# A forward transform by remainders of d mod 4, with a quarter of the frequencies in its tables, in a fused spectral and feed-forward kernel

## The chip, the cores and the metric

The kernel runs on one core of a Trainium2 chip. The metric is the device time of one execution in microseconds (us), here the median of three runs of the same program. A profile is one execution taken by the hardware profiler; its span is a little shorter than the measured time (1389.4 against 1391.22 us) and its inner times are used for the working. Engines are named as the profile names them: PE for the matrix engine's matmuls, PEld for its weight loads, DVE for the vector engine, ACT for the scalar engine, POOL for GpSimd, SP for the engine that issues most of the DMA transfers.

## The reference

Forward and backward of a gated mix of two branches over an input of 2048 rows (S) by 576 columns (D), bf16. Branch a multiplies the 2-D Fourier transform of `x` by learned weights and transforms back. Branch b is a feed-forward block with a gated GELU over 4608 inner columns.

```python
def _A_ref(x, w_r, w_i):
    X = jnp.fft.rfft2(x.astype(jnp.float32), axes=(-2, -1))
    X = X * (w_r + 1j * w_i)
    return jnp.fft.irfft2(X, s=(S, D), axes=(-2, -1)).astype(jnp.bfloat16)

def _B_ref(x, w_gate, w_up, w_down):
    return (_gelu(x @ w_gate) * (x @ w_up)) @ w_down

g = _sigmoid((x * gate_w).sum(-1, keepdims=True))
out = g * _A_ref(A_x, A_w_r, A_w_i) + (1 - g) * _B_ref(B_x, ...)   # with x = A_x for the gate
# ... and the gradients of out for A_x, A_w_r, A_w_i, the three B weights and gate_w
```

The change lies in the forward half of the spectral branch. There, `x` and the incoming gradient are both transformed: first over D (576 real points, of which the frequencies 0 to 288 are kept, so DF = 289), then over S.

## The kernel before

The kernel is one long stream of matmuls. The feed-forward block goes in 18 groups (`g`) of 256 inner columns, each in four pairs (`m`) of 512 rows. A pair computes `z` (the gradient times the down weight), `xy` (the input times the gate and up weights), and then the weight gradients of the group before it (`wps` matmuls, called jobs). Between those jobs, units of the spectral branch are dropped in one at a time by `fft_next()`; each takes a tile of the PSUM pool that `z` uses too, and that pool has one buffer.

The forward transform has two kinds of unit for each of 16 row groups `t` and each of two sources, so 32 of each. `u1` transforms over D by products with tables of cosines and sines. Even and odd `d` are kept apart (`par`), with half of the frequencies (HF = 145) in each table; the other half follows from sums and differences. `u2` transforms over a part of S and then forms those sums and differences on DVE.

```python
HF = 145
def eo(c):                      # columns of chunk c: even d for c = 0, 2, odd d for c = 1, 3
    return slice(256 * (c % 2) + c // 2, 256 * (c % 2) + 256, 2)
...
def u1(t):
    def f():
        yps = ps()
        for par, j in [(par, j) for par in range(2) for j in range(2)] + [(0, 2), (1, 2)]:
            ci, tab = (4, 4 + 2 * (t % 2) + par) if j == 2 else (2 * par + j, 2 * par + j)
            nc.tensor.matmul(yps[:, par, :2 * HF], lhsT=src[:, ci, t, :], rhs=tb.Dt[tab].rearrange("p c l -> p (c l)"),
                             start=(j == 0), stop=(j == 2))
        ys[t] = unit([2, 2, HF], name="Y")
        ...                     # ACT copies yps to Y, in bf16, with a scale for the gradient
def u2(t):
    def f():
        ...
        for o, ys_ in enumerate((Yf[:, 0:4:3, :], Yf[:, 2:0:-1, :])):
            nc.tensor.matmul(vps[:, o, :2 * HF]..., lhsT=R, rhs=ys_, start=True, stop=True)
        ve = unit([2, 2, HF], F32, name="ve")
        nc.scalar.copy(ve..., vps[:, :, :2 * HF])
        V.tensor_tensor(Vt[:, :, 0:HF], v[0], v[1], op=ALU.add)
        V.tensor_tensor(Vt[:, :, DF - 1:HF - 1:-1], v[0][:, :, 0:HF - 1], v[1][:, :, 0:HF - 1], op=ALU.subtract)
        LD.dma_start(dst[:, t], Vt[:])
```

The chunks of `d` are 128 + 128 + 128 + 128 + 64 columns; the last one, 512 to 575, has tables of its own (tabs 4 to 7), zero for the half of the partitions that belongs to the other row group of its pair. The order of `d` on the partitions is also that of the feed-forward weights: `load_w` brings `w_gate` and `w_up` in this order, and turns `w_down` by a transposing transfer into `wtmp`, from which four transfers within SBUF pick every second partition:

```python
def load_w(g, part, tails=LD):  # called with part 0, 1, 2 at the ends of pairs m = 0, 1, 2
    ...
    elif part == 1:
        wtmp[0] = wpool.tile([P, 4, FG], BF16, tag="wtmp", name="wtmp", bufs=1)
        ...
        LD.dma_start_transpose(wtmp[0][:], B_w_down[fsl, 0:512])
    else:
        ...
        for par in range(2):
            for h, r in enumerate((LO, HI)):
                LD.dma_start(wdT[r, 2 * par:2 * par + 2, :], wtmp[0][par:P:2, h:4:2, :])
```

Three places decide the order of emission that the change touches. `turned(h)` transposes eight tables `Rt`, and in its first call the two tables `B` as well, into the same PSUM tile; ACT copies the eight, DVE the two. `run_late(tb)` makes those `Rt` tables with sines on ACT, and from there on in that pair the results of the jobs are copied out by DVE. The pacing loop spreads the `n` spectral units of a pair evenly over its jobs:

```python
tables = {6: 1}.get(pr)         # pair 6: run_late ahead of job 1
for i, (w, f) in enumerate(jobs):
    if k < n and (at >= max(total * k / n - 0.45, free) or len(jobs) - i <= n - k):
        free = at + (1.7 if wide() else 0.0)
        fft_next()
        k += 1
    if i == tables:
        run_late(tb)
        wcopy[0] = VC
    f()
    at += w
```

The inverse transform has units `z` (`Z` and its copy `ZT`), `ztail` and `d`, sent by the same loop.

Of the kernel before, what the change touches and what calls it, by code (L numbers as in the profile page):

```python
# [10 lines left out]
ALU = mybir.AluOpType  # L11
# [29 lines left out]
HF = 145  # L41
NL = 2 * (HF - P)


def eo(c):

    return slice(256 * (c % 2) + c // 2, 256 * (c % 2) + 256, 2)
# [16 lines left out]
def iotas(nc, res, unit):  # L64
    tb = Tables()
    G, V = nc.gpsimd, nc.vector
    kw = dict(allow_small_or_imprecise_dtypes=True)
    tb.halfpi = res.tile([P, 1], F32, name="halfpi")
    V.memset(tb.halfpi[:], math.pi / 2)
    tb.pi = res.tile([P, 1], F32, name="pi")  # L70
    V.memset(tb.pi[:], math.pi * EPS_SCALE)
    tb.warm = res.tile([P, 1], F32, name="warm")
    nc.scalar.activation(tb.warm[:], tb.halfpi[:], ACT.Sin)
    tb.lrow = unit([HF], F32, name="lrow")
    G.iota(tb.lrow[:], pattern=[[1, HF]], base=0, channel_multiplier=0, **kw)
    tb.dcol = res.tile([P, 5], F32, name="dcol")
    for par in range(2):
        G.iota(tb.dcol[:, 2 * par:2 * par + 2], pattern=[[256, 2]], base=par, channel_multiplier=2, **kw)
    for r in (LO, HI):
        G.iota(tb.dcol[r, 4:5], pattern=[[0, 1]], base=512, channel_multiplier=1, **kw)  # L80
    tb.dn = res.tile([P, 5], F32, name="dn")
    V.tensor_scalar(tb.dn[:], tb.dcol[:], 1.0 / D, None, op0=ALU.mult)
    tb.late = []
    tb.Dt = []
    tb.Rt = []
    return tb


def iotas_R(nc, tb, res, unit):
    G, V = nc.gpsimd, nc.vector  # L90
    kw = dict(allow_small_or_imprecise_dtypes=True)
    tb.qcol_i = res.tile([P, 1], I32, name="qcol_i")
    G.iota(tb.qcol_i[:], pattern=[[0, 1]], base=0, channel_multiplier=1)
    kk = tb.kk = unit([2, P], F32, name="kk")
    tb.krow = kk[:, 0, :].rearrange("p (g k c) -> p g k c", k=2, c=2)
    for v in range(2):
        G.iota(tb.krow[:, :, v, :], pattern=[[1 - 2 * v, 32], [0, 2]], base=64 * v, channel_multiplier=0, **kw)
    G.memset(tb.krow[:, 0, 1, :], 32.0)
    tb.kadd = kk[:, 1, :].rearrange("p (k c) -> p k c", c=2)
    G.iota(tb.kadd, pattern=[[0, 64], [S // 4, 2]], base=S // 4, channel_multiplier=0, **kw)  # L100
    tb.scol = res.tile([P, T], F32, name="scol")
    G.iota(tb.scol[:], pattern=[[1, T]], base=0, channel_multiplier=16, **kw)
    par_i = res.tile([P, 1], I32, name="par_i")
    tb.par = res.tile([P, 2], F32, name="par_f")

    def parity():
        V.tensor_single_scalar(par_i[:], tb.qcol_i[:], 1, op=ALU.bitwise_and)
        V.tensor_copy(tb.par[:, 1:2], par_i[:])
        V.tensor_scalar(tb.par[:, 0:1], tb.par[:, 1:2], -1.0, 1.0, op0=ALU.mult, op1=ALU.add)
        V.tensor_scalar(tb.kadd[:, 0, 1:2], tb.par[:, 1:2], float(S // 2), float(S // 4), op0=ALU.mult, op1=ALU.add)  # L110
    return parity
# [7 lines left out]
def build_D(nc, tb, unit, c0, n):  # L119

    V = nc.vector
    step = 2.0 * math.pi / D
    TS = (nc.gpsimd if c0 else V).tensor_scalar
    X = unit([n, HF], F32, name="XD")
    y = unit([n, HF], F32, name="yD")
    for c in range(n):
        TS(y[:, c, :], tb.lrow[:], tb.dn[:, c0 + c:c0 + c + 1], MAGIC, op0=ALU.mult, op1=ALU.add)  # L130
    TS(y[:], y[:], -MAGIC, -float(D), op0=ALU.add, op1=ALU.mult)
    o = unit([n, 2, HF], name="Dt")

    def angles():
        for c in range(n):
            V.scalar_tensor_tensor(X[:, c, :], tb.lrow[:], tb.dcol[:, c0 + c:c0 + c + 1], y[:, c, :],
                                   op0=ALU.mult, op1=ALU.add)
        V.scalar_tensor_tensor(y[:], X[:], -1.0, X[:], op0=ALU.mult, op1=ALU.max)

    def sines():  # L140
        nc.scalar.activation(o[:, :, 0, :], y[:], ACT.Sin, bias=tb.halfpi[:], scale=-step)
        nc.scalar.activation(o[:, :, 1, :], X[:], ACT.Sin, scale=-step * EPS_SCALE)
        if c0 < 4:
            tb.Dt += [o[:, c] for c in range(n)]

    def tails():
        tl = unit([2, 2, 2, HF], name="Dt")
        nc.gpsimd.memset(tl[HI, 0], 0.0)
        nc.gpsimd.memset(tl[LO, 1], 0.0)
        for k, r in enumerate((LO, HI)):  # L150
            for par in range(2):
                V.tensor_scalar(tl[r, k, par], o[r, 0], tb.par[r, par:par + 1], None, op0=ALU.mult)
        tb.Dt += [tl[:, k, par] for k in range(2) for par in range(2)]
    return angles, sines, tails


# [99 lines left out]
def kernel(  # L256
# [23 lines left out]
    scr = [[dram.tile([4, P, FF], BF16, name=f"scr{k}_{m}") for m in range(T // 4)] for k in range(3)]  # L280
    a_scr = dram.tile([S, D], BF16, name="a_scr")
# [18 lines left out]
    def load_w(g, part, tails=LD):  # L300
# [4 lines left out]
        if part == 0:  # L305
            wgu = wts[g][0]
            for w, c0 in ((B_w_gate, 0), (B_w_up, FG)):
                cols = slice(c0, c0 + FG)
                LD.dma_start(wgu[:, 0:4, cols].rearrange("p (e k) f -> p e k f", e=2),
                             w[0:512, fsl].rearrange("(k p e) f -> p e k f", e=2, p=P))  # L310
                for r in (LO, HI):
                    tails.dma_start(wgu[r, 4, cols], w[512:D, fsl])
# [4 lines left out]
        else:  # L317
            wdT = wts[g][1]
            LD.dma_start(wdT[LO, 4, :], wdT[HI, 4, :])
            for par in range(2):  # L320
                for h, r in enumerate((LO, HI)):
                    LD.dma_start(wdT[r, 2 * par:2 * par + 2, :], wtmp[0][par:P:2, h:4:2, :])
# [282 lines left out]
    def fwd_units(src, dst, scale, ps=pftile):  # L605
        ys = {}

        def u1(t):
            def f():
                yps = ps()  # L610
                for par, j in [(par, j) for par in range(2) for j in range(2)] + [(0, 2), (1, 2)]:
                    ci, tab = (4, 4 + 2 * (t % 2) + par) if j == 2 else (2 * par + j, 2 * par + j)
                    nc.tensor.matmul(yps[:, par, :2 * HF], lhsT=src[:, ci, t, :], rhs=tb.Dt[tab].rearrange("p c l -> p (c l)"),  # L613
                                     start=(j == 0), stop=(j == 2))
                ys[t] = unit([2, 2, HF], name="Y")
                yo = ys[t][:].rearrange("p e c l -> p e (c l)")
                if scale is None:
                    nc.scalar.copy(yo, yps[:, :, :2 * HF])
                else:
                    nc.scalar.activation(yo, yps[:, :, :2 * HF], ACT.Copy, scale=scale[:, t:t + 1])  # L620
            return f

        def u2(t):
            def f():
# [3 lines left out]
                Yf = Y[:].rearrange("p e c l -> p (e c) l")  # L628
                for o, ys_ in enumerate((Yf[:, 0:4:3, :], Yf[:, 2:0:-1, :])):
                    nc.tensor.matmul(vps[:, o, :2 * HF].rearrange("p (e l) -> p e l", e=2), lhsT=R, rhs=ys_, start=True, stop=True)  # L630
                Vt = half([2, DF], name="Vt")
                ve = unit([2, 2, HF], F32, name="ve")
                nc.scalar.copy(ve[:].rearrange("p o c l -> p o (c l)"), vps[:, :, :2 * HF])
                v = [ve[:, 0], ve[:, 1]]
                V.tensor_tensor(Vt[:, :, 0:HF], v[0], v[1], op=ALU.add)
                V.tensor_tensor(Vt[:, :, DF - 1:HF - 1:-1], v[0][:, :, 0:HF - 1], v[1][:, :, 0:HF - 1], op=ALU.subtract)
# [4 lines left out]
    def tail_table():  # L641
# [4 lines left out]
        for k, r in ((2, P), (3, 32)):  # L646
            o = 512 * (k - 2)
            for c in range(2):
                nc.tensor.transpose(tp_[:, c, o:o + r], tb.Dt[k][0:r, c, 0:P], ident[0:r, 0:r])
            for c in range(2):  # L650
                nc.tensor.transpose(tp_[0:n, c, o + 256:o + 256 + r], tb.Dt[k][0:r, c, P:HF], ident[0:r, 0:r])
# [5 lines left out]
        for c in range(2):  # L657
            for e, sb in enumerate((tb.Dt[1], ot)):
# [5 lines left out]
    def turned(h):  # L664

        def f():
            tp_ = pftile(BF16)
            ts = range(8 * h, 8 * h + 8)
            for k, t in enumerate(ts):
                nc.tensor.transpose(tp_[:, 0, k * P:(k + 1) * P], tb.Rt[t], ident[:])  # L670
            o = unit([8, P], name="RT")
            nc.scalar.copy(o[:].rearrange("p t m -> p (t m)"), tp_[:, 0, :])
            if h == 0:
                for v in range(2):
                    nc.tensor.transpose(tp_[:, 1, v * P:(v + 1) * P], tb.B[:, v, :], ident[:])
# [160 lines left out]
    def inv_units(s, dv, scale):  # L836
# [14 lines left out]
        def z(p):  # L851
# [11 lines left out]
            f.wide = True  # L863
# [14 lines left out]
        def d(i):  # L878
            def f():
# [20 lines left out]
                LD.dma_start(dv[:, i, :], yo[:, 0:D])  # L900
            return f
# [18 lines left out]
    D0 = build_D(nc, tb, unit, 0, 2)  # L920
# [4 lines left out]
    D2 = build_D(nc, tb, unit, 2, 2)  # L925
    D2[0]()
    D4 = build_D(nc, tb, unit, 4, 1)
# [5 lines left out]
    titems(dB, dOT, 0, (None, None, phtile), (None, None, VC))[2]()  # L933
    D4[0]()
# [28 lines left out]

    def wide():
        return hasattr(next(u for u in fft[fft_pos[0]:] if not getattr(u, "noslot", False)), "wide")
# [48 lines left out]
    for g in range(NG):  # L1014
# [3 lines left out]
        for m in range(NPR):  # L1018
# [65 lines left out]
            else:  # L1084
# [32 lines left out]
                tables = {6: 1}.get(pr)  # L1117
                for i, (w, f) in enumerate(jobs):
                    if k < n and (at >= max(total * k / n - 0.45, free) or len(jobs) - i <= n - k):
# [20 lines left out]
            if m < 3 and g + 1 < NG:  # L1140
                load_w(g + 1, m)
# [247 lines left out]
```

## Time and profile before

| | |
|---|---|
| time, median of 3 (lowest to highest) | 1391.22 us (1391.06 to 1391.48) |
| span of the profiled execution | 1389.4 us, 26,012 instructions |
| granted PE clock | 1.0 of full speed all along |
| the 40 slices of the span | PE at nine tenths or more in every one |
| DMA, mean | 154 GB/s, 214.49 MB moved |
| where the forward transform lies | from 74 to 298 us (first `u1` matmul to last `Vt`) |

In the profile's rows `u1`'s matmuls are those of line L613 (`pf<-Dt`), `u2`'s those of L630, the jobs' L552, L570 and L584, `z`'s L424 and L429, `xy`'s L433 and L440, and the second half of the kernel, products with stored tiles, is L1239. Matmuls overlap one another in the array[...]. What one costs in a stream is the distance from its start to the start of the next, and the timeline gives that.

### The profile page before, as it was taken

To read this page: it belongs to the slowest core of one execution; us is meant where nothing else is said; L and a number is where in the kernel's file an instruction comes from. 1 tells how busy PE (TensorE), PEld (TensorE's weight loads), DVE (VectorE), ACT (ScalarE), POOL (GpSimd) and SP (SyncE) were. 2 spreads that over 40 slices of the span, in tenths; PEclk is the share of its full clock that TensorE was granted. 3 is DMA by queue.
4 is the path that set the end of the run, shared out by engine and by line. 5 is a ranking of instruction groups with operands and counts; after the bars stand their busy time and mean duration, and the time that the engine had idled before them with its cause. 6 is when DMAs were issued, how large, how long until landed. Compare 5 with 4: busy or idle time off the path is not lost.

```text
span 1389.4 us, 26012 instructions
## 1 busy us (share of the span) xinstructions
PE 1380.2 (99%) x10272; PEld 912.9 (66%) x10272; DVE 752.9 (54%) x1419; ACT 702.3 (51%) x1299; POOL 245.2 (18%) x486
## 2 busy tenths in 40 slices
PE   9999999999999999999999999999999999999999
PEld 7556556556556566556566566556777777777777
DVE  7976556555888877885767676560001742121111
ACT  7976767767878778866767666651000000000000
POOL 3001110123345634422110111110000110000000
PEclk9999999999999999999999999999999999999999
DMA  7424344355466556555556555759999998777773
GB/s 225 120 85 135 114 128 106 103 157 142 126 158 161 157 147 162 140 142 136 141 151 157 147 158 150 168 124 281 190 192 203 224 193 168 162 159 166 156 151 89
DMA packets 510791, 214.49 MB, mean 154 GB/s; under 512 B 312555, under 2 KB 503725, under 8 KB 510669
## 3 DMA queue, kind: packets, MB, share of 16 engines
q1 hardware_dynamic: 493546, 187.44, 58.0%
q0 software_dynamic: 14912, 24.24, 6.5%
q8 instruction: 80, 1.31, 0.4%
q10 hardware_dynamic: 2210, 1.15, 0.3%
q14 instruction: 43, 0.34, 0.1%
HBM read 41.05 MB, written 93.84 MB: 97 GB/s over the span
## 4 chain that ended last, share of the span: by engine, by line
PE 95%; DVE 3%; ACT 2%; issue 0%; POOL 0%; DVEq 0%; POOLq 0%; ACTq 0%
PE acc L1239 30%; PE xy L440 17%; PE wps L570 17%; PE wps L552 9%; PE z L424 9%; PE wps L584 2%; PE xy L433 2%; PE pf L613 2%; PE z L429 2%; PE pf L886 1%; PE pf L812 1%; PE pf L630 1%; PE pf L723 1%; PE pf L888 1%; PE pf L859 1%; PE pf L379 0%
## 5 line engine op out<-in xcount | busy, mean ns | idle before, releaser
L1239 PEld LDWEIGHTS <-pin 128*128 128x128 bf16 x3456 | 337.6, 98 | 86.2 <-issue 0.5
L570 PE MATMUL wps<-dH,xn 128*128 128x512 bf16 x1152 | 271.4, 379 | 1.1 <-DVE dwd L521 1.0
L440 PE MATMUL xy<-wgu,xT 128*128 128x512 bf16 x1152 | 270.6, 380 | 0.0
L440 PEld LDWEIGHTS <-xT 128*128 128x128 bf16 x1152 | 106.5, 98 | 132.8 <-issue 24.8
L570 PEld LDWEIGHTS <-xn 128*128 128x128 bf16 x1152 | 111.4, 98 | 119.7 <-issue 1.9
L1256 ACT COPY bo<-acc 128x288 f32<-128x288 f32 x32 | 12.7, 398 | 305.1 <-PE acc L1239 271.6
L552 PE MATMUL wps<-dB,A 128*128 128x288 bf16 x1152 | 153.8, 286 | 0.1
L577 POOL DMA_DIRECT2D out_dram<-dw x134 | 72.8, 547 | 431.1 <-ACT dw L521 390.0
L1239 PE MATMUL acc<-wgT,pin 128*128 128x288 bf16 x1152 | 143.8, 286 | 0.0
L1239 PE MATMUL acc<-wuT,pin 128*128 128x288 bf16 x1152 | 143.6, 286 | 0.0
L1239 PE MATMUL acc<-wd_all,pin 128*128 128x288 bf16 x1152 | 142.6, 286 | 0.0
L424 PE MATMUL z<-wdT,dOT 128*128 128x256 bf16 x1152 | 137.7, 273 | 0.6 <-ACT ZT L862 0.2
L552 PEld LDWEIGHTS <-A 128*128 128x128 bf16 x1152 | 112.1, 98 | 33.2 <-issue 0.3
L452 ACT ACTIVATE da<-z,omg 128x256 bf16<-128x256 f32 x288 | 112.0, 471 | 32.4 <-PE z L429 32.3
L424 PEld LDWEIGHTS <-dOT 128*128 128x128 bf16 x1152 | 112.3, 98 | 22.9 <-issue 1.7
L461 ACT CAST xb<-xy 128x512 bf16<-128x512 f32 x144 | 85.0, 590 | 49.8 <-PE xy L440 49.8
L1311 DVE SCALAR_TENSOR_TENSOR f32t<-gwf,dlog,b16t 128x576 f32<-128x576 f32 x16 | 13.1, 817 | 170.4 <-DMA b16t<-dxa_scr 170.4
L459 ACT ACTIVATE q<-xy 128x512 bf16<-128x512 f32 x144 | 87.8, 613 | 15.8 <-PE xy L440 14.5
L462 ACT CAST hu<-xy 128x512 bf16<-128x512 f32 x144 | 87.4, 607 | 0.0
L498 DVE TENSOR_TENSOR xb<-xb,sg 128x1024 bf16<-128x1024 bf16 x48 | 33.2, 691 | 94.3 <-ACT sg L490 94.2
L521 ACT CAST dw<-wps 128x512 bf16<-128x512 f32 x72 | 42.3, 589 | 55.4 <-PE wps L570 53.1
L1270 DVE SCALAR_TENSOR_TENSOR b16t<-b16t,g,f32t 128x576 bf16<-128x576 bf16 x16 | 13.1, 818 | 98.3 <-DMA b16t<-a_scr 98.1
(224 smaller groups left out, 1655.6 us busy)
## 6 DMA issues: line engine op xcount, KB each, us to landing
scr<-dH SPq DMA_DIRECT2D x144, 256.0 KB, 3.4
scr<-A SPq DMA_DIRECT2D x72, 256.0 KB, 2.5
out_dram<-dw POOLq DMA_DIRECT2D x134, 64.0 KB, 2.5
wd_all<-in_B_w_down_dram SPq DMA_DIRECT2D x3, 1728.0 KB, 9.4
out_dram<-dwd POOLq DMA_DIRECT2D x34, 144.0 KB, 3.1
scr_p<-Vt SPq DMA_DIRECT2D x32, 145.0 KB, 3.0
wgu<-in_B_w_gate_dram SPq DMA_DIRECT2D x18, 256.0 KB, 4.3
wgu<-in_B_w_up_dram SPq DMA_DIRECT2D x18, 256.0 KB, 3.3
```

The source lines that it names most:

```text
L424: nc.tensor.matmul(zo(t), lhsT=dOT[:, ci, t, :], rhs=wdT[:, ci, :], start=(t % 4 < 2 and ci == 0), stop=False)
L440: nc.tensor.matmul(xy[k][:, t % 2, :], lhsT=xT[:, ci, t, :], rhs=wgu[:, ci, :], start=False, stop=(ci == 3))
L452: nc.scalar.activation(da[:, t, :], z[:, t % 2, t // 2, :], ACT.Copy, scale=omg32[:, 4 * m + t:4 * m + t + 1])
L459: nc.scalar.activation(q[:, h, :], xy[:, :, 0:FG], ACT.Square)
L461: nc.scalar.copy(xb[:, h, :], xy[:, :, 0:FG])
L462: nc.scalar.copy(hu[:, h, :], xy[:, :, FG:2 * FG])
L498: V.tensor_tensor(xb[:], xb[:], s[:], op=ALU.mult)
L521: wcopy[0](out, in_)
L552: nc.tensor.matmul(wps[:, :288], lhsT=tl(0, t)[:, fch * P:(fch + 1) * P], rhs=dB[:, t, h * 288:(h + 1) * 288], start=(t == 0), stop=(t == ...
L570: nc.tensor.matmul(wps[:].rearrange("p a b -> p (a b)"), lhsT=xn[:, t, c * P:(c + 1) * P], rhs=kt[t // 4][1][:, t % 4].rearrange("p k f -> ...
L577: wst[0].dma_start(ov[:, c, fsl], dw[:, k, :])
L1239: nc.tensor.matmul(acc[:, :288], lhsT=src[:, r, :], rhs=w_of(r)[:, h * 288:(h + 1) * 288], start=(first and r == 0), stop=(last and r == F ...
```

## The change

The forward transform over D is rewritten so that the columns are sorted by `d mod 4` (`r` = 0, 1, 2, 3), and each table holds only a quarter of the frequencies (QF = 73). From the four remainders the frequencies l, 288 − l, 144 − l and 144 + l follow by sums and differences. Remainders 0 and 2 share one PSUM bank with their cosines and sines placed in crossed order, and so do 1 and 3, so that `u1` has four matmuls over a quarter (2 × 73 columns) and two over the tail chunk (4 × 73 columns, zeros where the remainder is another). `u2`'s two matmuls keep their form; its sums and differences take five DVE instructions where there were two, by way of a new fp32 tile `M`.

```diff
 HF = 145
+QF = 73
 def eo(c):
-    return slice(256 * (c % 2) + c // 2, 256 * (c % 2) + 256, 2)
+    return slice(c, 512, 4)
...
 def u1(t):
-                for par, j in [(par, j) for par in range(2) for j in range(2)] + [(0, 2), (1, 2)]:
-                    ci, tab = (4, 4 + 2 * (t % 2) + par) if j == 2 else (2 * par + j, 2 * par + j)
-                    nc.tensor.matmul(yps[:, par, :2 * HF], lhsT=src[:, ci, t, :], rhs=tb.Dt[tab].rearrange("p c l -> p (c l)"),
-                                     start=(j == 0), stop=(j == 2))
-                ys[t] = unit([2, 2, HF], name="Y")
+                for o in range(2):
+                    for r, bs in ((2 * o, slice(0, 4, 3)), (2 * o + 1, slice(1, 3))):
+                        nc.tensor.matmul(yps[:, o, 0:4 * QF].rearrange("p (b l) -> p b l", b=4)[:, bs, :], lhsT=src[:, r, t, :],
+                                         rhs=tb.D4[:, r], start=(r % 2 == 0), stop=False)
+                for o in range(2):
+                    nc.tensor.matmul(yps[:, o, 0:4 * QF], lhsT=src[:, 4, t, :],
+                                     rhs=tb.D4t[:, t % 2, o].rearrange("p b l -> p (b l)"), start=False, stop=True)
+                ys[t] = unit([2, 4 * QF], name="Y")
...
 def u2(t):
-                for o, ys_ in enumerate((Yf[:, 0:4:3, :], Yf[:, 2:0:-1, :])):
-                    nc.tensor.matmul(vps[:, o, :2 * HF].rearrange("p (e l) -> p e l", e=2), lhsT=R, rhs=ys_, start=True, stop=True)
+                for o in range(2):
+                    nc.tensor.matmul(vps[:, o, 0:4 * QF], lhsT=R, rhs=Y[:, o], start=True, stop=True)
...
-                V.tensor_tensor(Vt[:, :, 0:HF], v[0], v[1], op=ALU.add)
-                V.tensor_tensor(Vt[:, :, DF - 1:HF - 1:-1], v[0][:, :, 0:HF - 1], v[1][:, :, 0:HF - 1], op=ALU.subtract)
+                V.tensor_tensor(M[:, 0]..., ve[:, 0:4]..., ve[:, 4:8]..., op=ALU.add)
+                V.tensor_tensor(M[:, 1, 0], ve[:, 0:2], ve[:, 4:6], op=ALU.subtract)
+                V.tensor_tensor(M[:, 1, 1], ve[:, 6:2:-3], ve[:, 2:8:5], op=ALU.subtract)
+                up = Vt[:, :, 0:2 * (HF - 1)]...[:, :, :, 0:QF]
+                dn = Vt[:, :, DF - 1:0:-1]...[:, :, :, 0:QF - 1]
+                V.tensor_tensor(up, M[:, :, :, 0], M[:, :, :, 1], op=ALU.add)
+                V.tensor_tensor(dn, M[:, :, :, 0, 0:QF - 1], M[:, :, :, 1, 0:QF - 1], op=ALU.subtract)
```

The inverse transform still needs tables over even and odd `d`. So three such tables (columns 5 to 7 of `dcol`, 3 × 145) are built beside the four quarter ones (4 × 73), and their angles are now made wholly on POOL. The tail tables are 16 products of 64 × 73 on POOL, where there were four of 64 × 290 on DVE.

The order of `d` on the partitions changes for the feed-forward weights too. A partition now holds four neighbouring rows of the weight, and `w_down` gets there by way of a scratch in device memory, in one part more, and one pair later:

```diff
+    wscr = [dram.tile([512, FG], BF16, name=f"wscr{k}") for k in range(2)]
...
-                LD.dma_start(wgu[:, 0:4, cols].rearrange("p (e k) f -> p e k f", e=2),
-                             w[0:512, fsl].rearrange("(k p e) f -> p e k f", e=2, p=P))
+                LD.dma_start(wgu[:, 0:4, cols], w[0:512, fsl].rearrange("(p r) f -> p r f", r=4))
...
-            for par in range(2):
-                for h, r in enumerate((LO, HI)):
-                    LD.dma_start(wdT[r, 2 * par:2 * par + 2, :], wtmp[0][par:P:2, h:4:2, :])
+            LD.dma_start(wscr[g % 2][:].rearrange("(c p) f -> p c f", p=P), wtmp[0][:])
+        else:
+            LD.dma_start(wts[g][1][:, 0:4, :], wscr[g % 2][:].rearrange("(p r) f -> p r f", r=4))
...
-                load_w(g + 1, m)
+                for part in ((0, 1), (2,), (3,))[m]:
+                    load_w(g + 1, part)
```

Three changes concern the order of emission alone: the transposes of `B` move to the second call of `turned`; the sines of pair 6 come ahead of job 2, not job 1; and in the pacing loop the last unit of a pair may be sent earlier, so that some job time (2.0 for the units `z` and `d` of the inverse transform) is left behind it.

```diff
-            if h == 0:
+            if h == 1:
                 for v in range(2):
                     nc.tensor.transpose(tp_[:, 1, v * P:(v + 1) * P], tb.B[:, v, :], ident[:])
...
-                tables = {6: 1}.get(pr)
+                last = getattr(upcoming(n - k0)[-1], "last", 0.0) if n > k0 else 0.0
+                tables = {6: 2}.get(pr)
                 for i, (w, f) in enumerate(jobs):
-                    if k < n and (at >= max(total * k / n - 0.45, free) or len(jobs) - i <= n - k):
+                    if k < n and (at >= max(min(total * k / n - 0.45, total - last - 0.9 * (n - 1 - k)), free) or len(jobs) - i <= n - k):
```

The number of PE instructions stays the same (10,272 matmuls, each with its weight load).

## The prediction

> **What bounds the kernel now.** I read the busy line of the page first, then the waits of PE, then the timeline of PE.
>
> ```profile
> PE 1380.2 (99%) x10272; PEld 912.9 (66%) x10272; DVE 752.9 (54%) x1419; ACT 702.3 (51%) x1299; POOL 245.2 (18%) x486
> ```
>
> PE is busy for 99% of the span; DVE and ACT for about half. A busy PE need not be one at its peak, so the next question is whether it waits. The waits of PE (engine, line, waited for: total us, times, longest):
>
> ```profile
> PE pf L914 <- POOL ident masks.py:199: 1.4, 1, 1.4
> PE pf L675 <- ACT RT L672: 1.1, 1, 1.1
> PE wps L570 <- DVE dwd L521: 1.0, 1, 1.0
> PE pf L723 <- ACT Xg L728: 0.5, 1, 0.5
> PE pf L613 <- ACT ve L633: 0.4, 2, 0.2
> PE z L424 <- ACT ZT L862: 0.2, 1, 0.2
> PE pf L379 <- DVE dOT L386: 0.2, 1, 0.2
> ```
>
> Together 4.8 us of 1389. So the time is the length of the matmul stream, and only two things shorten it: fewer columns through the array, or these few waits gone. The timeline of PE shows what a unit takes in the stream (start, duration of the merged piece, count at the end; I use the distances between starts):
>
> ```profile
> 87.29 0.91 PE L613 MATMUL pf<-Dt,xT 128*128 128x290 bf16 x6
> 88.04 1.02 PE L440 MATMUL xy<-wgu,xT 128*128 128x512 bf16 x4
> 88.90 1.03 PE L570 MATMUL wps<-dH,xn 128*128 128x512 bf16 x4
> ...
> 654.97 0.23 PE L886 MATMUL pf<-Dt,ZT 128*128 128x145 bf16 x1
> 655.03 0.23 PE L886 MATMUL pf<-Oi,ZT 128*128 128x145 bf16 x1
> 655.10 0.29 PE L888 MATMUL pf<-At,ZU 68*128 68x290 bf16 x1
> 655.23 0.23 PE L886 MATMUL pf<-Dt,ZT 128*128 128x145 bf16 x1
> ```
>
> A `u1` of six matmuls takes 88.04 − 87.29 = 0.75 us, 125 ns for each 290 columns. Four of 512 take 0.86 us, 215 ns each. The inverse transform already has matmuls of half the width, each with new weights: two of 145 columns take 655.10 − 654.97 = 0.13 us, 65 ns each, and one of 290 takes 0.13. So narrow matmuls with a fresh weight load still cost by their columns.
>
> **What the Trainium skill says.** "TensorE: Matmul & The Clock Gate", section "Back-to-back issue gap", gives a warm gap of N/2.4 + 2.5 ns for N columns: 63 ns for 145 and 123 for 290, and the trace agrees (65 and 125). The same section says that a real stream with weight loads is slower, about 81 ns for 128 columns; here eight of 128 columns (L859) take from 651.93 to 652.38 on the timeline, 56 ns each, so I go by the trace. "PSUM — Partial Sum Buffer", "The four PSUM rules", says that the first matmul of a group clears the written-marks of its whole bank, and later ones overwrite where no mark is set. That is why one start flag for each bank is enough in the new `u1`, although its second remainder writes other columns: no extra matmul is needed. No view of a trace shows these marks. "VectorE: DVE Perf Modes", on the trn2 errata, gives (N + 151)/0.96 ns for an fp32 addition of two tensors; for `u2`'s 290 and 288 elements that is 459 and 457 ns, and the trace has 460 and 452 (lines below). "ScalarE: Activation LUTs", "What ACT_TABLE_LOAD costs", has about 1283 ns for a load; the trace has 1.28 us for each, at 77.25 and at 81.52.
>
> **The change part by part.**
>
> 1. `u1`, on the path. Before: 6 × 290 = 1740 columns, 0.75 us. After: 4 × 146 + 2 × 292 = 1168 columns. By the trace's neighbours: 4 × 65 ns + 2 × 126 ns = 0.51 us. Saved 0.24 us in each of 32 units: **7.7 us**. `u2`'s 292 columns for 290, in 64 matmuls, at (215 − 125)/222 = 0.4 ns a column, give back 0.05 us.
>
> 2. `u2`'s sums on DVE, beside the path. The groups of DVE between 74 and 300 us:
>
> ```profile
> L635 DVE TENSOR_TENSOR Vt<-ve 128x290 bf16<-128x290 f32 x32 | 14.7, 460 | 39.4 <-ACT ve L633 36.8 <-DMA wtmp<-in_B_w_down_dram 2.2
> L636 DVE TENSOR_TENSOR Vt<-ve 128x288 bf16<-128x288 f32 x32 | 14.4, 452 | 0.0
> ```
>
> Each `u2` has 0.91 us of DVE now, and DVE comes to it idle (36.8 us of waiting for `ve`). After: sums over 292, 146, 146, 292 and 288 elements. With the section's formula that is an estimate of 461 + 309 + 309 + 461 + 457 = 2.0 us, so 1.09 more in each, 35 us in all. The windows from 74 to 313 us have DVE busy for 145.9 of 239 us, 61%; with 35 more 76%. Only the transfer of `Vt` waits for these sums, and `Vt`'s readers come much later. I count nothing for it on the path.
>
> 3. ACT copies 584 columns where it copied 580. Nothing.
>
> 4. The sines of pair 6. On the timeline the 32 matmuls of L552 start at 75.24 and the next line follows at 80.37, after the wait on the DVE copy `dwd`. 32 of them need 3.9 us elsewhere (8 in 0.98), so 1.2 us are lost. ACT is in its sines from 77.25 to 81.52, and DVE, which takes both copies meanwhile, is in a run of table and GELU work until 79.86. With the sines one job later, ACT copies the first result ahead of them and its buffer is free for L570: **1.2 us**.
>
> 5. `turned`. The eight transposes of L670 start at 300.79 and need 0.45 us, but L675 starts at 302.50, after ACT's copy of `RT` (301.44 to 302.45), which reads the same tile: 1.26 us lost. After the change four jobs of 0.86 us lie between, from 301.24 to 302.10; the second `turned` then needs the one PSUM buffer, still read until 302.45, so some 0.4 us stay. Saved **0.85 us**.
>
> 6. The last unit of a pair. Comparing the orders of the matmuls, beside `u1` and `turned` only five pairs of the inverse transform change, by one job's shift of a unit. They hold three visible losses, where `z` comes soon after a unit on its buffer: 780.53 to 781.79 for four of 512 (0.86 needed), and 793.87 to 795.13 and 807.66 to 808.93 for eight of 288 (0.98 needed). That is 0.40 + 0.28 + 0.29, together **1.0 us**.
>
> 7. The opening, 0 to 35 us. DVE loses 1.0 us of tail products and two of its angle steps; it gains one absolute value over 3 × 145. POOL gains three rows of angles, by its rows (145 wide 0.42 us each, 290 wide 0.44) some 4.5 us in all, done near 7 us, while DVE wants them after 8.1. ACT's sines of 290 become 435, so the gate's sigmoid comes some 0.4 us later. I take the balance as zero, with half a microsecond either way. The 16 tail products on POOL are wanted only at 74 us.
>
> 8. The weights by way of `wscr`: two transfers for four, issued one pair (12 us) ahead of `z`, where a landing takes 2.7 us. Hidden.
>
> Sum: −7.7 + 0.05 − 1.2 − 0.85 − 1.0 = −10.7 us. Moved units tend to make some new small wait, and the opening may lose a little; I leave 0.6 us for that. 1391.2 − 10.1 = **1381.1 us**.
>
> **The rivals.** (a) *DVE becomes the limit*: its sums delay the GELU products that stand behind them in its queue, and through them the jobs. For it: 76% is much, and the queue is in order. Against it: the products of a pair feed jobs of the next group, four pairs later, and PE waits for DVE only once in the trace outside the opening. It would give back 2 to 6 us, so about 1384 to 1387. (b) *The saved columns turn into waits*: `u1` and `u2` share one PSUM buffer, and ACT's copies of 0.64 to 0.74 us set when it is free; four jobs of 0.86 us between units just cover that. In the trace a unit waits there seldom (0.4 us for L613). A shorter `u1` doesn't shorten the cover, since the jobs between stay. Were each of 32 units to lose 0.1 us, 3 us would go: 1384. (c) *The narrow matmuls are bound by weight loads* of 98 ns each: then 4 × 98 + 2 × 126 = 0.64 us, and only 3.4 us are saved: 1385. The 65 ns of L886, with loads of its own, speaks against it. (d) *Opening or weights come late*: a stall of POOL's angles holds DVE's `xT` copies and PE for 1 to 2 us. (e) *Everything moves well*: all waits of parts 4 to 6 vanish and the opening gains: 1379.5.
>
> **Range and chances.** The middle is 1381.1. (e) sets the lower side, with some extra room; (a) to (d), each of perhaps one chance in ten, the upper: 1378 to 1386. Two per cent are 27.8 us, nearly three times the whole sum, so neither verdict of 2% is likely: 0.01 for faster, 0.98 for within, 0.01 for slower.
>
> **What would show it.** `u1`'s group in the timeline at 0.50 to 0.52 us from start to the next (c wrong); PE's busy time lower by about 8; the waits on `dwd` and of L675 gone, a wait of the second `turned` of about 0.4 in their place; DVE at some 76% between 74 and 300 with no PE wait on it (a wrong); ACT idle ahead of `ve` as before (b wrong). The prediction is wrong if PE shows new waits on DVE or on `ve`, if the narrow matmuls take 80 ns or more, or if the first 35 us grow by over 1 us.

## The result, and the profile after

The changed kernel takes 1384.03 us (1383.99 to 1385.74) against 1391.14 us on the same chips: a ratio of 0.9952, 95% interval 0.9939 to 0.9965. That is 7.1 us less; the prediction's middle was 10.1 less. The range holds it, but 3 us of the expected gain are missing, and the question is where.

The busy line of the page after, and the longest waits of PE in it:

```profile
PE 1363.2 (99%) x10186; PEld 908.5 (66%) x10272; DVE 783.2 (57%) x1514; ACT 701.6 (51%) x1300; POOL 259.8 (19%) x513
```

```profile
PE xy L460 <- issue: 6.8, 43, 0.2
PE pf L943 <- POOL ident masks.py:199: 1.4, 1, 1.4
PE pf L651 <- ACT Y L640: 1.1, 1, 1.1
PE pf L633 <- ACT ve L655: 1.0, 2, 0.7
PE pf L399 <- DVE dOT L406: 0.8, 1, 0.8
...
PE pf L697 <- ACT RT L702: 0.2, 1, 0.2
```

Two things must be read with care. This profile has 10,186 matmul records where the program has 10,272; 69 of the missing ones are `xy` matmuls of L460. A missing record looks like an idle engine, and the first line, 43 times 0.16 us ahead of L460, is of that kind: the distance from start to start at those places is that of the matmuls before and one unseen. Two later profiles (that of the iotas sent first, and that of pair 7's own `q` with the sines put back, both below) have all 10,272 records, and there this line is gone. For the same reason PE's busy time in this profile can't be compared with that of before. What can be compared are the starts of the same matmuls. I take the first `z` matmul of each of the 72 pairs (L424 before, L444 after) from the two timelines:

| start of pair (us) | before | after | difference | what lies in between |
|---|---|---|---|---|
| 0 | 7.86 | 7.73 | −0.13 | first loads |
| 3 | 36.98 | 37.74 | +0.76 | the opening |
| 6 | 66.56 | 67.38 | +0.82 | |
| 7 | 82.09 | 81.47 | −0.62 | pair 6: sines moved, one `u1` |
| 8 | 94.10 | 94.77 | +0.68 | pair 7: two `u1` |
| 22 | 289.32 | 283.45 | −5.86 | 0.46 less in nearly every pair, each with two `u1` |
| 23 | 305.65 | 298.92 | −6.73 | `turned` |
| 59 | 767.95 | 761.31 | −6.65 | |
| 62 | 808.93 | 801.35 | −7.57 | the last units, three pairs |
| 71 | 922.99 | 915.68 | −7.31 | 0.26 given back in pair 64 |

From there to the last matmul nothing changes. Nearly all of the gain of the narrow tables is there (7.2 us of 7.65), and so are those of `turned` and of the last units. Two places are worse than expected: pair 2, and pair 7 above all. The timeline of PE in pair 7, after:

```profile
86.67 0.43 PE L633 MATMUL pf<-Dt,xT 128*128 128x146 bf16 x4
86.93 0.41 PE L636 MATMUL pf<-Dt,xT 128*128 128x292 bf16 x2
87.18 1.02 PE L460 MATMUL xy<-wgu,xT 128*128 128x512 bf16 x3
88.05 1.03 PE L590 MATMUL wps<-dH,xn 128*128 128x512 bf16 x4
90.14 0.41 PE L651 MATMUL pf<-Y,Rt 128*128 128x292 bf16 x2 [1.07 <-ACT Y L640]
90.39 1.02 PE L590 MATMUL wps<-dH,xn 128*128 128x512 bf16 x4
92.16 0.42 PE L633 MATMUL pf<-Dt,xT 128*128 128x146 bf16 x4 [0.75 <-ACT ve L655]
```

The new `u1` takes 87.18 − 86.67 = 0.51 us. But the four jobs of 512 columns, which need 0.86, are followed by `u2` only 2.09 us after their start, and the next four by `u1` after 1.77. So 1.23 and 0.91 us are lost. Before, only the second place lost anything, 0.39:

```profile
89.77 0.41 PE L630 MATMUL pf<-Y,Rt 128*128 128x290 bf16 x2
90.02 1.03 PE L570 MATMUL wps<-dH,xn 128*128 128x512 bf16 x4
91.27 0.91 PE L613 MATMUL pf<-Dt,xT 128*128 128x290 bf16 x6 [0.22 <-ACT ve L633]
```

That makes 1.75 us of new waiting. ACT at that time, and the first and last of the DVE run that it waits for:

```profile
82.67 1.28 ACT L507 ACT_TABLE_LOAD   x1
83.97 1.06 ACT L507 ACTIVATE s<-s 128x1024 bf16<-128x1024 bf16 x1
84.93 1.55 ACT L472 ACTIVATE da<-z,omg 128x256 bf16<-128x256 f32 x4
86.35 0.60 ACT L481 CAST xb<-xy 128x512 bf16<-128x512 f32 x1
86.82 0.62 ACT L482 CAST hu<-xy 128x512 bf16<-128x512 f32 x1
88.96 0.60 ACT L479 ACTIVATE q<-xy 128x512 bf16<-128x512 f32 x1 [1.52 <-DVE xb L524]
89.45 0.64 ACT L640 CAST Y<-pf 128x584 bf16<-128x584 f32 x1
```

```profile
85.06 0.69 DVE L518 TENSOR_TENSOR xb<-xb,s 128x1024 bf16<-128x1024 bf16 x1 [1.94 <-ACT s L507]
...
88.17 0.69 DVE L524 TENSOR_TENSOR xb<-xb,q 128x1024 bf16<-128x1024 bf16 x1
```

ACT does not lack time here: it stands idle for 1.5 us ahead of `q`, until DVE's L524 has read the squares of the pair before, because `q` has one buffer. `Y`, which `u2` needs, is behind `q` in ACT's queue. L524 is late because it ends a run of six DVE instructions that waits for the sigmoid (L507), and the sigmoid is late because the sines went later.

### The profile page after: what moved, and what is told of

Same layout as the page of the kernel before. It is cut to its first block, busy times and chain, and to the rows that moved or that the text cites. A ratio compares the mean times of both kernels' runs of the same rounds, so it can differ in the third digit from the quotient of the medians.

```text
span 1382.2 us, 25988 instructions
## 1 busy us (share of the span) xinstructions
PE 1363.2 (99%) x10186; PEld 908.5 (66%) x10272; DVE 783.2 (57%) x1514; ACT 701.6 (51%) x1300; POOL 259.8 (19%) x513
## 4 chain that ended last, share of the span: by engine, by line
PE 92%; ACT 3%; DVE 2%; DMA 1%; issue 1%; ACTq 0%; SPq 0%; DVEq 0%
PE acc L1273 31%; PE wps L590 16%; PE xy L460 16%; PE wps L572 10%; PE z L444 8%; PE wps L604 2%; PE xy L453 2%; PE z L449 2%; DMA wgu<-in_B_w_up_dram 1%; DMA xn<-in_A_x_dram 1%; PE pf L914 1%; PE pf L840 1%; PE pf L751 1%; PE pf L633 1%; PE pf L916 1%
## 5 line engine op out<-in xcount | busy, mean ns | idle before, releaser
L460 PE MATMUL xy<-wgu,xT 128*128 128x512 bf16 x1083 | 258.6, 380 | 8.2 <-issue 6.8
L460 PEld LDWEIGHTS <-xT 128*128 128x128 bf16 x1152 | 106.4, 98 | 132.9 <-issue 24.8
L444 PE MATMUL z<-wdT,dOT 128*128 128x256 bf16 x1152 | 137.7, 273 | 0.0
L444 PEld LDWEIGHTS <-dOT 128*128 128x128 bf16 x1152 | 112.3, 98 | 21.6 <-issue 0.6
```

The lines of the kernel that those rows point to most:

```text
L444: nc.tensor.matmul(zo(t), lhsT=dOT[:, ci, t, :], rhs=wdT[:, ci, :], start=(t % 4 < 2 and ci == 0), stop=False)
L460: nc.tensor.matmul(xy[k][:, t % 2, :], lhsT=xT[:, ci, t, :], rhs=wgu[:, ci, :], start=False, stop=(ci == 3))
```

## The experiments

The first theory (1) is therefore: moving the sines does not take their delay away, it passes it on, by way of the sigmoid, DVE's products and the single `q`. Its rival (2): the new transform makes those waits, by longer sums on DVE or a shorter `u1`. For the opening, theory P blames the tail products on POOL, its rival DVE's own order.

**The new transform with the old orders.** `turned`, the sines and the pacing as they were:

```diff
-                tables = {6: 2}.get(pr)
+                tables = {6: 1}.get(pr)
...    # turned: transposes of B under h == 0; pacing without `last`
```

> The changed kernel with its three changes of order undone, so the new transform alone. The narrower u1 saves 0.23 us in each of 32 units by the changed kernel's trace, 7.4 us; the opening loses 0.8. Theory 1 (moving the sines of pair 6 only passes their delay on to pair 7, so that it gains nothing): pair 7 loses little here, pair 6 keeps its wait of about 1.2 us, and the time is 1384.3 to 1385.0, at most 1 us above the changed kernel's 1384.0. Theory 2 (the new waits of pair 7, 1.8 us, come from the new transform itself, by way of its longer sums on DVE or its shorter u1): pair 7 still waits 1.5 us or more, and the time is about 1386.5.

Measured: 1384.95 us. Pair 6 keeps its wait, which also swallows the 0.23 us of its narrower `u1` (the pair is as long as before), and pair 7 has no wait on `Y`; the waits of PE:

```profile
PE wps L590 <- DVE dwd L541: 1.3, 1, 1.3
PE pf L702 <- ACT RT L699: 1.1, 1, 1.1
PE pf L399 <- DVE dOT L406: 0.8, 1, 0.8
...
PE pf L633 <- ACT ve L655: 0.5, 2, 0.2
```

Against (2). The three orders together are worth 0.9 us in the changed kernel, where the prediction had 3.05.

**The orders alone, on the kernel before.**

> The kernel before with the three changes of order alone; the transform, its tables and the weights' order stay. Theory 1: pair 6 gains 1.2 us, pair 7 loses it again in waits of u2 and u1 on ACT; what stays is the transposes' 0.85 and about 0.7 of the last units: 1389.4 to 1390.2. Theory 2: pair 7 has no new wait, and the gain is 1.2 + 0.85 + 0.7 = 2.75 us, 1388.4.

Measured: 1389.91 us (before 1391.19; ratio 0.9992, interval 0.9983 to 1.0001, so not clear of no change). By the starts of the pairs, pair 6 gains 1.21 us and pair 7 loses 1.51, with nothing of the new transform in the program. PE in pair 7:

```profile
89.24 0.41 PE L630 MATMUL pf<-Y,Rt 128*128 128x290 bf16 x2 [0.83 <-ACT Y L618]
89.48 1.02 PE L570 MATMUL wps<-dH,xn 128*128 128x512 bf16 x4
91.25 0.91 PE L613 MATMUL pf<-Dt,xT 128*128 128x290 bf16 x6 [0.74 <-ACT ve L633]
```

This rules (2) out as the source of the wait. The new transform adds at most the quarter microsecond between 1.51 and 1.75.

**The sines back, the rest of the change kept.**

```diff
-                tables = {6: 2}.get(pr)
+                tables = {6: 1}.get(pr)
```

> The changed kernel with one of the orders undone: the sines of pair 6 come ahead of job 1 again. Theory 1: pair 6 loses 1.2 us, pair 7 gains 1.2 to 1.8 back, the time is 1383.3 to 1384.1. Theory 2: pair 7 keeps its 1.8 us and the time rises by 1.2 to 1385.2.

Measured: 1383.78 us, within theory 1 and no slower than the changed kernel. Pair 6 is 1.44 us longer than there and pair 7 1.75 shorter. Taken by itself, the move of the sines brought nothing.

**A second buffer for `q` in pair 7.** The link of the chain itself:

```diff
-            tiles = [ewt(tag, g) for tag in ("xb", "q", "hu")]
+            tiles = [ewt(tag, 0 if tag == "q" and pr == 7 else g) for tag in ("xb", "q", "hu")]
```

> The changed kernel with one more buffer: in pair 7 the tile q (the squares) does not reuse the one that pair 6's GELU products still read. Theory 1, its chain (late sines, late sigmoid, late products on DVE, so ACT waits 1.5 us to write q, and Y behind it in ACT's queue comes late for u2): ACT's wait for q and PE's wait of 1.1 us for Y go, the wait for ve stays or halves, and the time falls by 1.2 to 1.6 us to about 1382.6. Rival (ACT's backlog of work alone delays Y, whatever q waits for): PE's waits stay at 1.5 us or more in sum, the time at 1383.7 or above.

Measured: 1382.41 us. PE's matmuls stand in the same order as in the changed kernel; pair 7 is 1.63 us shorter. PE, then ACT:

```profile
88.10 1.03 PE L590 MATMUL wps<-dH,xn 128*128 128x512 bf16 x4
88.97 0.41 PE L651 MATMUL pf<-Y,Rt 128*128 128x292 bf16 x2
89.22 1.02 PE L590 MATMUL wps<-dH,xn 128*128 128x512 bf16 x4
90.60 0.42 PE L633 MATMUL pf<-Dt,xT 128*128 128x146 bf16 x4 [0.35 <-ACT ve L655]
```

```profile
87.36 0.64 ACT L479 ACTIVATE q<-xy 128x512 bf16<-128x512 f32 x1
87.85 0.69 ACT L640 CAST Y<-pf 128x584 bf16<-128x584 f32 x1
```

`u2` follows its four jobs after 0.87 us, without a wait, although the sines and the sigmoid are as late as they were (84.02 us for L507); ACT writes `q` without a wait, and `Y` comes 1.6 us sooner. So the buffer was the link. To see whether the sines' move is worth its 1.2 us once that link is open, they were put back with the buffer kept:

> The kernel with pair 7's own q, and with the sines of pair 6 ahead of job 1 as they were before the change. If moving the sines is worth its 1.2 us as soon as the buffer behind it is free, this is 1.0 to 1.4 us slower than with the sines moved: 1383.4 to 1383.8, about the time with the shared q (1383.8). If the own buffer alone is what helps, it stays at 1382.4.

Measured: 1383.62 us, 1.2 more; pair 6 is 1.44 us longer than with the sines moved, pair 7 0.13 shorter. The move and the buffer pay only together: of the four combinations, three take 1383.6 to 1384.0, the fourth 1382.4.

**The tail products one pair later.**

```diff
         parity()
-        D4[2]()
...
                 elif m == 1:
                     next(makeB)
+                    D4[2]()
```

> The changed kernel with the 16 tail products on POOL sent after the iotas of the B tables, one pair later. Theory P (the products take 9.9 us on POOL and push those iotas to 29 us, where one of them holds up a DVE scalar operation, 1.12 instead of 0.43 us, in a queue that PE waits on at 34 us): the wait on dOT falls from 0.8 to about 0.2 us, the time falls by 0.7 us to 1383.3. Rival (the loss comes from DVE's own order in the opening, its angle steps ahead of the xT copies): no change, 1384.0.

Measured: 1383.15 us; pair 2 loses 0.04 where it lost 0.67. POOL in the changed kernel shows how the products came into the way, and DVE what they met there:

```profile
13.93 9.92 POOL L173 TENSOR_SCALAR Dt<-Dt,r_f 64x73 bf16<-64x73 bf16 x16
...
29.05 0.87 POOL L243 IOTA k2B<- 128x128 f32 x1
```

```profile
28.37 0.68 DVE L521 TENSOR_TENSOR q<-xb,q 128x1024 bf16<-128x1024 bf16 x1
29.09 1.12 DVE L523 TENSOR_SCALAR xb<-s 128x1024 bf16<-128x1024 bf16 x1
30.24 0.69 DVE L524 TENSOR_TENSOR xb<-xb,q 128x1024 bf16<-128x1024 bf16 x1
```

L243 is an iota, an instruction that fills a tile with index numbers. L523 takes 0.42 to 0.45 us at all its other places; here it ends 0.3 us after the iota does. Before, the iota ran at 25.40. But the tail products had also pushed some fifteen short column operations into that time. To tell them apart, the iotas were sent ahead of those, the products left where they are:

```diff
-    k_, nt, a0, a1, b1, m0, m1 = tb.bcols
...                                 # the iotas
     yield
+    k_, nt, a0, a1, b1, m0, m1 = tb.bcols
...
                     build_R(nc, tb, unit, 4)
+                    next(makeB)
                     columns_B(nc, tb, res)
-                elif m == 1:
-                    next(makeB)
```

> The changed kernel with the tail products where they are and the four iotas of the B tables sent ahead of POOL's short column operations instead of behind them. Theory I (it is the 0.9 us iota that holds up the DVE scalar operation of 1.12 us at 29 us): that operation takes 0.43 us again, the wait on dOT falls to 0.2, the time to about 1383.3. Rival (any POOL work at that moment does it, here the short column operations): the operation stays long or another one becomes long, the time stays at 1384.0.

Measured: 1383.62 us, between the two forecasts; the wait on `dOT` is 0.2 us. Its profile's first `z` stands 0.73 us later than in the changed kernel, which is the landing of the first loads (PE waits 1.0 us for the gradient there) and differs from profile to profile; from pair 2 to pair 3 it gains 0.68. POOL and DVE in it:

```profile
24.42 0.87 POOL L242 IOTA k2B<- 128x128 f32 x1
...
29.70 2.56 POOL L216 TENSOR_TENSOR bcol<-bcol 128x1 f32<-128x1 f32 x4
```

```profile
29.60 0.43 DVE L523 TENSOR_SCALAR xb<-s 128x1024 bf16<-128x1024 bf16 x1
```

The column operations now lie beside L523 and leave it alone; it was the iota.

**DVE's sums, less and more.** Without the first three of the five instructions (the sums and differences `M` are left out, so the transform's values are others), and with those three done twice:

```diff
-                V.tensor_tensor(M[:, 0]..., ve[:, 0:4]..., ve[:, 4:8]..., op=ALU.add)
-                V.tensor_tensor(M[:, 1, 0], ...)
-                V.tensor_tensor(M[:, 1, 1], ...)
+                Mv = ve[:].rearrange("p (k v u) l -> p k v u l", k=2, v=2)   # up and dn read Mv
```

> The changed kernel without the first three of u2's five DVE instructions: the sums and differences M are left out and the last two work on ve itself, so the transform's values are not the reference's. DVE does 29 us less. Theory H (u2's sums are hidden beside the matmuls): the time stays within 0.2 us of 1384.0. Rival D (DVE holds back part of the gain): the time falls by 1 us or more, below 1383.

Measured: 1383.72 us. That is 0.3 less, a little outside the 0.2 of theory H and far from rival D. No pair from 2 to 28 is longer or shorter than the changed kernel's by more than 0.04, and the last pair starts at 915.68 us in both profiles. What the profiled execution gained, 0.45 us of its span, lies behind the last matmul, where the programs are the same (3.12 us to the end against 3.56), so the sums that were left out did not bring it.

> The changed kernel with the first three of u2's five DVE instructions done twice, with the same result; DVE does 29 us more, some 88 per cent of its stage. Theory H: there is still room, the time rises by less than 0.5 us. Rival D: DVE is at its limit, waits on it appear on PE, and the time rises by 2 us or more.

Measured: 1385.85 us, 1.8 more, which fits neither theory as written. In the profiled execution (1385.48 us) the starts of the pairs show 1.34 in a single pair, pair 8, and none in the 14 after it that carry the same extra work. The windows from 74 to 300 us (PE, PEld, DVE, ACT, POOL busy, then clock, DMA share, GB/s), the changed kernel first, then this one:

```profile
74.00:300.00 226.00, 221.56 (x1582) 136.38 (x1602) 172.44 (x363) 168.65 (x307) 27.48 (x51) 1.00 0.43 123
```

```profile
74.00:300.00 226.00, 220.39 (x1571) 135.33 (x1591) 196.82 (x458) 168.01 (x307) 26.07 (x48) 1.00 0.43 121
```

DVE at 76% and at 87% of the stage holds back none of those 14 pairs. In pair 8 the same waits come again, on `Y` and `ve`:

```profile
103.25 0.41 PE L651 MATMUL pf<-Y,Rt 128*128 128x292 bf16 x2 [0.66 <-ACT Y L640]
103.50 1.02 PE L590 MATMUL wps<-dH,xn 128*128 128x512 bf16 x4
105.27 0.42 PE L633 MATMUL pf<-Dt,xT 128*128 128x146 bf16 x4 [0.75 <-ACT ve L655]
```

The link is again the single `q`. DVE and ACT in pair 8, in the changed kernel:

```profile
99.67 0.69 DVE L524 TENSOR_TENSOR xb<-xb,q 128x1024 bf16<-128x1024 bf16 x1
```

```profile
100.46 0.60 ACT L479 ACTIVATE q<-xy 128x512 bf16<-128x512 f32 x1
```

And with the sums done twice:

```profile
101.27 0.69 DVE L524 TENSOR_TENSOR xb<-xb,q 128x1024 bf16<-128x1024 bf16 x1
```

```profile
102.06 0.60 ACT L479 ACTIVATE q<-xy 128x512 bf16<-128x512 f32 x1 [1.46 <-DVE xb L524]
```

The sums stand ahead of L524's run in DVE's queue. With three of them left out, L524 ends 0.75 us before ACT takes `q` (99.57 and 100.32), in the changed kernel 0.1 us before, and with them done twice ACT has to wait. The delay of the sines is not the reason, since with the old orders L524 also ends 0.1 us before `q` in this pair (100.05 and 100.14). Pair 8 is the last in which two products for later use (L516, L517) stand ahead of L524; the kernel sends them behind it for groups from 2 on. In pair 9 of the changed kernel L524 ends 1.6 us before `q` (110.35 and 111.92). Whether a second `q` would free pair 8 was not tried.

**Both repairs together**, the later tail products and pair 7's own `q`:

> The changed kernel with the tail products one pair later and with pair 7's own q. If the two losses are independent: 0.8 less for the first and 1.2 to 1.6 less for the second, so 1381.6 to 1382.1. If one shift only hands its wait on to the next pair, as the sines did: 1382.5 or more.

Measured: 1381.91 us (ratio to before 0.9934, interval 0.9919 to 0.9949). Pair 2 is 0.63 and pair 7 1.63 us shorter than in the changed kernel, so the two losses were independent. This version is 2.1 us faster than the changed kernel, and stands within a microsecond of the prediction's middle.

## Why the prediction was right or wrong

| step | predicted (us) | measured (us), by starts |
|---|---|---|
| 1, `u1` narrower, `u2` two columns wider | −7.65 | −0.23 in nearly every one of 32 units, −7.2 |
| 4, sines of pair 6 | −1.2 | −1.2 in pair 6, +1.75 in pair 7 |
| 5, `turned` | −0.85 | −0.86 |
| 6, last units | −1.0 | −0.93, then +0.26 in pair 64 |
| 7, the opening | 0 ± 0.5 | +0.8, 0.67 of it in pair 2 |
| left for new small waits | +0.6 | counted in the rows above |
| sum | −10.1 | −7.3 (start of pair 71) |

- **Step 1** was right, and with it the reading that narrow matmuls with fresh weights cost by their columns: rival (c) is out (0.51 us for a unit, not 0.64).
- **Step 2** was right: DVE's share came out at 76%, the five instructions at 0.46 + 0.31 + 0.31 + 0.46 + 0.46 us, 2.0 as estimated, and leaving out 28 us of DVE work in that stage (172.44 to 144.46) moved no pair from 2 to 28. Rival (a) cost nothing in the changed kernel. But the run with twice the first sums shows how near it was: slack is not a share of a stage, and in pair 8 the sums had left 0.1 us of it.
- **Step 4 failed.** It found the right wait and the right way to remove it, and stopped there. It asked when ACT's first copy would be done and not what else comes 1.1 us later when the sines do. ACT's sines, the sigmoid, six DVE instructions and the single `q` are one chain, and PE stands at its end some 10 us on. In the kernel before, PE's 1.2 us of waiting in pair 6 gave that chain the time it needed. The allowance of 0.6 us for new small waits did not cover the 1.75. One of the signs that the prediction had named as speaking against it did appear: PE's waits on `ve` grew from 0.4 to 1.0 us, beside the new 1.1 on `Y`. Rival (b) had named the place, ACT's copies and the one PSUM buffer, but with the wrong reason and spread over all units; it occurred in one pair only. That the time came out at (b)'s 1384 is chance. That it lies in the range at all rests on step 1, by far the largest part, and on the width of the range.
- **Steps 5 and 6** were right to a tenth of a microsecond, also in the 0.4 us that stay at the second `turned` (it starts 1.27 us after four jobs that need 0.86). The 0.26 us given back in pair 64 come from the orders too, since the orders alone give back 0.27 there, and were not foreseen.
- **Step 7 failed** in its sum. POOL's angles were done at 8.45 us and not near 7, but that was just in time; DVE took them at 8.48. What cost time was dismissed in one sentence: the tail products are indeed wanted only at 74 us, but the prediction did not ask what stands behind them in POOL's queue, nor how long they take (9.9 us). They pushed the iota onto L523, which grew by 0.7 us, and PE's wait on `dOT` rose from 0.2 to 0.8.
- **Step 8** was right: no step between pairs shows a wait on the weights.
- The busy time of PE, named as a sign to look for (8 us less), fell by 17 us in the profile with the missing records. In the two later profiles that have all of them it reads 1372.2 and 1372.1 us against 1380.2 before, 8 less as predicted.

Not settled is where the spread of the changed kernel's runs (two of six at 1385.3 and 1385.7) comes from. The profiles show the first `z` anywhere from 7.1 to 8.5 us, as the first loads land, which moves the whole run by less than that; whether this is the cause was not tried.

## What to carry to other kernels

When a wait on the bounding engine is taken away by moving work later, follow everything that the moved work feeds, by queue order and by buffer reuse, to the next place where the bounding engine meets it: the wait may have been the pause that this chain needed. Two changes that are each worth almost nothing alone can be worth something together, as the later sines and the second `q` were (1.4 us, 1383.78 to 1382.41). And compare two long traces by the starts of the same instructions, stage by stage: here that placed the gains and losses pair by pair, where busy times and lists of waits did not.

## What the runs showed of the hardware

- A POOL iota of 0.87 us (128 x 128, fp32) held up a bf16 scalar operation of DVE (128 x 1024, in SBUF) that started 0.04 us after it: 1.12 us instead of 0.43. In the kernel before, the same iota ran beside two copies of DVE out of PSUM (from 25.40 us), and these took 1.02 us, as elsewhere. POOL's scalar and tensor operations beside the same DVE scalar operation did not hold it (0.43 us in the runs with the tail products later and with the iotas first). Their own times varied. The 16 tail products took 9.92 us at one place and 13.44 at another, each 64 x 73 one between 0.46 and 0.97 us in the changed kernel, and four tensor operations of 128 x 1 took 1.00 us in the kernel before, 1.89 in the changed one and 2.56 in the run with the iotas first.
- Four matmuls of 146 columns, each with new weights and two of the outputs in two separate runs of 73, went at 65 ns each: neither the weight load (98 ns by its record) nor the split output showed in the stream, where the undivided 145 columns of the inverse transform also go at 65 ns.
